# Last opening head unit in halves, low bits by a shift, four resident word tiles, and another order of the second product, in a retention and two-MLP kernel

## The chip, the cores and the metric

One core of a Trainium2 chip. The metric is the device time of one launch in microseconds (us). The kernel before was run three times: 565.46, 564.31 and 565.28 us, median 565.28. TensorE is PE below, its weight load PEld, VectorE DVE, ScalarE ACT, SyncE SP; SP issues most of the transfers.

## The reference

All in fp32, on 2 batches, 8 heads, 768 steps, 64 channels a head; then on 1536 tokens of 512, with 2048 hidden units in each MLP.

```python
for t in range(S):                                   # a decay for each head
    state = gamma * state + einsum('bhd,bhe->bhde', k[:, :, t], v[:, :, t])
    y[:, :, t] = scale * einsum('bhd,bhde->bhe', q[:, :, t], state)
x = y.transpose(0, 2, 1, 3).reshape(1536, 512)
h = x @ moe_w_in;  x = softplus(h) @ moe_w_out       # the first MLP
h = x @ moe2_w_in; x = (h * clip(h + 3, 0, 6) / 6) @ moe2_w_out   # the second
```

## The kernel before, in words

**Exact products from rounded parts.** PE multiplies a rounded fp32 type. Each fp32 operand is cut into a high part (rounded, a copy on ACT) and a low part (what is left, a subtraction on DVE), and each product is three matmuls into one PSUM bank: w high by x high, w high by x low, w low by x high.

**Weights.** A weight tile comes as pairs of 32-bit words (class `Words`, l. 344 to 403). `fetch` loads 512 KB into a `raw` slot by SP. Then `made` (l. 392) records these steps: `bits` (ACT: the low bits of the first words, by an activation), `sign` (ACT), `scale` (ACT) with `clamp` (DVE), or `scaled` and `capped` (both DVE) in their place, and `merge` (DVE). The result is a tile of words in a `cv` slot. `weight` (l. 405) goes on with `high` (ACT) and `low` (DVE) into a `w` slot. The 32 tiles of the first MLP are numbered in the order of their use: in0, in1, in2, out0 (number 3), in3, out1, in4, out2 and so on; `BY_ACT(n)` (l. 180) says which have `scale` on ACT. The first eight in-tiles have their words stored to DRAM (256 KB each) and loaded again by `early_in` (l. 480), for sums of weights that later products use.

**Retention.** `attend` (l. 610) makes one head unit of 128 steps of one batch: load k, q, v; transpose k and q (PE); `kT` (ACT) and `qT` (DVE); `vs` (DVE); the scores (16 matmuls into two banks); two masks (DVE, `pw`); the product of `vs` and k for the state `st`; `carry` (what the state gives); the copy `seen` (DVE), which stands between `carry` and the inner product into the same banks; `inner` (16 matmuls); and the split into `x_hi` (ACT) and `x_lo` (DVE). Units 0 to 3 (START is 4) are the opening; they make the first 512 tokens (c = 0). The other units run in pairs between the matrix products.

**The MLP.** `gemm1` (l. 858) makes 128 hidden rows of 512 tokens, 12 matmuls; for its first step G1(0) all of x high runs ahead of all of x low. ACT copies the bank to `g`, softplus gives `hi` (ACT) and `lo` (DVE). `gemm2` (l. 996) adds the products with a tile of `w_out` into four banks: 4 groups of three matmuls. G1(n) and G2(n) below are the n-th of each. For c = 1 and 2, and in the second MLP, sums of weights and of tokens are multiplied instead, by a scheme with fewer products.

**The order.** Nothing is issued where it stands in the code. `Plan` (l. 25 to 136) is a list planner: each step is a task with an engine, a cost, a due time, the slots it takes and gives, and for a transfer a load on the queue. It runs the tasks in a simulated time; the engine that can start first takes, among its tasks that can start then, the one due first. All instructions are recorded by one line, so every row of the profile says L45, and tiles are told apart by name. A change to one cost can move steps anywhere.

Of the kernel before, what the change touches and what calls it, by code (L numbers as in the profile page):

```python
# [10 lines left out]
F32 = mybir.dt.float32  # L11
# [7 lines left out]
P = 128  # L19
# [126 lines left out]
def kernel(ctx, tc, q, k, v, w1_in, w1_out, w2_in, w2_out, table, out):  # L146
# [33 lines left out]
    def BY_ACT(n):  # L180
        return n < 4 or n >= 16

# [161 lines left out]
    class Words:  # L344


        def __init__(self, m, key, src, inside=0):
            self.m, self.key, self.src = m, key, src
            self.raw_k, self.cv_k = (f"raw{m}", key), (f"cv{m}", key)

        def raw(self):
# [39 lines left out]

        def made(self, at, fetch_at, load, give, by_act=False, hold=0.0):
# [12 lines left out]
    def weight(o, f, number):  # L405
# [204 lines left out]
    def attend(u):  # L610
# [47 lines left out]

        def ps(x):
            return slice(x * NP // parts, (x + 1) * NP // parts)  # L660

        def turned(n, x):
            def go():
                for p in range(NP)[ps(x)]:
                    nc.tensor.transpose(bank((n + "P", u))[:, p, :], tile_of(n)[:, 2 * p:2 * p + 2, :].rearrange("s h d -> s (h d)"), ident)
# [5 lines left out]
        for x in range(parts):  # L671
            at = x and 0.1
            tp = task("PE", cost["Tk"] / parts, turned("k", x), [ik[x], ready.get(("S", u - 2))], d["Tk"] + at, take=[] if x else [("bank", ("kP", u))])
            kt.append(task("ACT", ACP if parts == 1 else act(NP * C // parts, True), lambda x=x: nc.scalar.activation(tile_of("kT")[:, ps(x)], bank(("kP", u))[:, ps(x)], AF.Copy), [tp], d[S] - 1.0 + at,
                           take=[] if x else own("kT"), give=[("kP", u)]))
            tp = task("PE", cost["Tq"] / parts, turned("q", x), [iq[x], ready.get(("C", u - 2))], d["Tq"] + at, take=[] if x else [("bank", ("qP", u))], give=[("q", u)])
            qt.append(task("DVE", PSX if parts == 1 else dve(NP * C // parts), lambda x=x: nc.vector.tensor_tensor(tile_of("qT")[:, ps(x)], bank(("qP", u))[:, ps(x)], tq_sb[:, ps(x)], ALU.mult), [tp, ready["q"]],
                           d[S] - 1.1 + at, take=[] if x else own("qT"), give=[("qP", u)]))
# [57 lines left out]

        s = [task("PE", cost["S0"] / parts, lambda x=x: all_scores(x), [kt[x], qt[x]], d["S"] + x / 10, take=[] if x else [("bank", x) for x in sc], give=[("kT", u)] + [("qT", u)] * first) for x in range(parts)]
        pt = [task("DVE", PSX, masked(g), s, d["I"] - 1.8 + g * 0.6, take=[] if g else own("pw"), give=[sc[g]]) for g in range(2)]
        dp = task("PE", cost["D0"], product, [vs, *ik], d["D"], take=[("bank", dk)], give=[("k", u)])
# [4 lines left out]
        else:  # L744
# [3 lines left out]
            n = task("DVE", 0.1, between, [c], d["C"] + 0.5)  # L748
        c = task("PE", cost["I0"], inner, pt + [vs, n], d["I"], take=[("bank", y) for y in o] if first else [],
                 give=[("pw", u), ("vs", u)])  # L750
        def x_at(part):
            return x_of(part, 0)[:, :, u * C:(u + 1) * C].rearrange("p (y i) t -> p y i t", y=2)

        need = min(due["G1", 0], d["I"] + 12.0)
        o2 = task("ACT", PSX, lambda: nc.scalar.activation(x_at("hi"), split_out(), AF.Copy), [c], need - 1.5, give=o)
        o3 = task("DVE", PSX, lambda: nc.vector.tensor_tensor(x_at("lo"), split_out(), x_at("hi").bitcast(F32), ALU.subtract), [o2],
                  need - 0.8, give=o)
        ready["x", u] = [o2, o3]

# [98 lines left out]
    def gemm1(s):  # L858
# [7 lines left out]

        def go(only=(0, 1)):
            h = at_slot(("h", s))
            w = at_slot(("w", (m, 0, f))).rearrange("p a (k n) -> p a k n", k=KD)
            ops = [(kk, a, b) for kk in range(KD) for a, b in ((0, 0), (0, 1), (1, 0))]  # L870
            for n, (kk, a, b) in enumerate(sorted(ops, key=lambda x: x[2]) if s == 0 else ops):
                if b in only:
                    nc.tensor.matmul(h, w[:, a, kk, :], x_part(kk, b), start=(n == 0), stop=(n == 3 * KD - 1))
# [122 lines left out]
    def gemm2(s):  # L996
# [238 lines left out]
```

## Time and profile before

| | before |
|---|---|
| median of three runs | 565.28 us (564.31 to 565.46) |
| the profiled execution | 564.72 us, of it the span 562.8 |
| PE busy | 553.3 us, 98% |
| PE weight load busy | 473.3 us, 84% |
| DVE busy | 440.5 us, 78% |
| ACT busy | 367.1 us, 65% |
| granted clock of PE | 1.00 over the span |
| transfers | 100.51 MB, 179 GB/s |

The span is the profiled part of the execution, and 1.9 us lie around it. A group's row in the page tells how long its engine was idle just before its instructions, and which engine's instruction or which transfer ended that idle time. Times in the timelines are from the span's start. Matmuls overlap: a row of 12 ends later than the next one starts, so spacing is read from start to start.

### The profile page before, as it was taken

How to read it: one execution, taken by the hardware profiler on the slowest of the kernel's cores; microseconds unless marked ns; L12 is line 12 of the kernel's file. 1: busy time of each engine (PE TensorE's matmuls, PEld its weight loads, DVE VectorE, ACT ScalarE, POOL GpSimd, SP SyncE). 2: the span in 40 equal slices, each digit the busy share in tenths (PEclk: the TensorE clock that was granted, in tenths of full speed). 3: DMA queues.
4: the chain of work that ended last, by engine and by line, in shares of the span. 5: the costliest groups of instructions: out<-in, count | busy, mean ns of one | idle time of the engine just before them, and what ended most of it. 6: DMA issues, size and time to landing. Idle time of an engine off the chain costs nothing.

```text
span 562.8 us, 9577 instructions
## 1 busy us (share of the span) xinstructions
PE 553.3 (98%) x3685; PEld 473.3 (84%) x3685; DVE 440.5 (78%) x778; ACT 367.1 (65%) x600; POOL 5.8 (1%) x13
## 2 busy tenths in 40 slices
PE   8899999999999999999999999999999999999996
PEld 6687788888788888888888999988998889988895
DVE  5999998889799778999998775837887897854443
ACT  4697999997774536687968734448778775432220
POOL 0000000000000000000000000000000000000000
PEclk9999999999999999999999999999999999999999
DMA  9997999994422216988907522243755752236003
GB/s 208 286 238 257 285 294 285 324 236 158 151 75 76 75 62 205 323 305 281 358 21 279 187 75 76 82 180 112 229 183 186 272 177 76 75 106 231 1 0 113
DMA packets 80829, 100.51 MB, mean 179 GB/s; under 512 B 41360, under 2 KB 58000, under 8 KB 80784
## 3 DMA queue, kind: packets, MB, share of 16 engines
q1 hardware_dynamic: 79776, 98.45, 54.3%
q0 software_dynamic: 720, 1.31, 1.3%
q8 instruction: 29, 0.48, 0.3%
q10 hardware_dynamic: 288, 0.14, 0.1%
q14 instruction: 16, 0.13, 0.1%
HBM read 74.98 MB, written 23.59 MB: 175 GB/s over the span
## 4 chain that ended last, share of the span: by engine, by line
PE 82%; DVE 5%; ACT 5%; DMA 5%; issue 1%; DVEq 0%; ACTq 0%; SPq 0%
PE banks L45 82%; DMA raw<-in_moe_w_in_dram 3%; ACT cv L45 2%; DMA raw<-in_moe_w_out_dram 1%; DVE g L45 1%; DVE cv L45 1%; DVE raw L45 1%; DVE lo L45 1%; DMA stash_out<-raw 1%; ACT hi L45 1%; ACT raw L45 0%; DVE qT L45 0%; DMA out_dram<-ob 0%; ACT between L45 0%; ACT w L45 0%
## 5 line engine op out<-in xcount | busy, mean ns | idle before, releaser
L45 PE MATMUL banks<-w,parts 128*128 128x512 f32 x579 | 136.7, 390 | 0.0
L45 PEld LDWEIGHTS banks<-w,parts 128*128 128x128 f32 x579 | 108.0, 188 | 21.3
L45 PE MATMUL banks<-hi,w 128*128 128x512 f32 x384 | 124.8, 393 | 0.0
L45 PE MATMUL banks<-xf,w 128*128 128x384 f32 x672 | 123.2, 337 | 0.4 <-DVE c L45 0.4
L45 PEld LDWEIGHTS banks<-xf,w 128*128 128x128 f32 x672 | 118.3, 188 | 3.4 <-DVE c L45 0.7
L45 PEld LDWEIGHTS banks<-hi,w 128*128 128x128 f32 x384 | 72.1, 188 | 15.0
L45 PE MATMUL banks<-xl,w 128*128 128x512 f32 x342 | 81.0, 391 | 0.2
L45 PEld LDWEIGHTS banks<-xl,w 128*128 128x128 f32 x342 | 63.7, 188 | 14.1 <-DVE hs L45 0.5
L45 PE MATMUL banks<-lo,w 128*128 128x512 f32 x192 | 75.1, 391 | 0.2 <-DVE lo L45 0.2
L45 ACT ACTIVATE e<-c,three 128x384 f32<-128x384 f32 (+1 forms) x32 | 24.6, 770 | 47.0 <-DVE c L45 46.5
L45 ACT ACTIVATE cv<-raw,half 128x512 uint32<-128x512 uint32 x64 | 48.6, 761 | 7.5 <-DMA raw<-in_moe_w_out_dram 3.7
L45 ACT ACTIVATE cv<-raw 128x512 f16<-128x512 int32 x64 | 50.0, 788 | 1.2
L45 DVE SCALAR_TENSOR_TENSOR cv<-raw,cv 128x512 uint32<-128x512 uint32 x64 | 44.1, 690 | 1.4
L45 PE MATMUL banks<-x_hi,w 128*128 128x512 f32 x128 | 42.5, 399 | 1.0 <-ACT x_hi L45 1.0
L45 PEld LDWEIGHTS banks<-lo,w 128*128 128x128 f32 x192 | 36.1, 188 | 7.9 <-DVE lo L45 0.9
L45 DVE TENSOR_SCALAR raw<-raw 128x512 f32<-128x512 f32 x76 | 32.3, 430 | 11.4 <-ACT raw L45 10.5
L45 ACT ACTIVATE hi<-g 128x512 fp32r<-128x512 f32 x48 | 29.9, 626 | 16.7 <-PE banks L45 10.1
L45 DVE TENSOR_TENSOR lo<-g,hi 128x512 fp32r<-128x512 f32 x48 | 33.0, 688 | 8.0 <-ACT hi L45 7.8
L45 ACT ACTIVATE parts<-c 128x768 fp32r<-128x768 f32 x32 | 26.9, 842 | 18.6 <-DVE c L45 18.6
L45 DVE TENSOR_TENSOR parts<-c,parts 128x768 fp32r<-128x768 f32 x32 | 30.6, 957 | 10.2 <-ACT parts L45 9.9
L45 ACT ACTIVATE e<-e 128x512 f32<-128x512 f32 x48 | 29.7, 624 | 9.3 <-DVE e L45 9.2
L45 ACT ACTIVATE raw<-raw 128x512 f32<-128x512 f32 x52 | 34.4, 668 | 0.7
(95 smaller groups left out, 653.5 us busy)
## 6 DMA issues: line engine op xcount, KB each, us to landing
raw<-in_moe_w_in_dram SPq DMA_DIRECT2D x32, 512.0 KB, 5.6
raw<-in_moe_w_out_dram SPq DMA_DIRECT2D x32, 512.0 KB, 5.7
w<-stash_out SPq DMA_DIRECT2D x32, 512.0 KB, 5.4
stash_out<-raw SPq DMA_DIRECT2D x16, 512.0 KB, 3.4
w<-parts_out SPq DMA_DIRECT2D x14, 512.0 KB, 5.4
parts_out<-w SPq DMA_DIRECT2D x8, 512.0 KB, 4.3
stash_h<-hs SPq DMA_DIRECT2D x16, 256.0 KB, 2.3
g<-stash_h SPq DMA_DIRECT2D x16, 256.0 KB, 4.6
```

Of the source, the lines that this page charges most:

```text
L45: return self.plan.tc.keep_in_program_order(getattr(self.engine, op)(*args, **kwargs))
```

## The change

It has five parts. (1) The last opening unit (u = 3) is made in halves: scores, masks, inner product, `x_hi` and `x_lo`; G1(0)'s part of x high runs in two steps of four matmuls. (2) Tiles 3 to 11 and 16 to 31 get their low bits by a shift on DVE (`shifted`) and not by ACT's `bits`; all tiles have `scale` on ACT. (3) The words of in0 to in3 stay in four SBUF tiles (`words`); their stores and reloads go. (4) In `gemm2` the three products come as (w high, hi), (w low, hi), (w high, lo), and for c = 0 as two PE tasks: eight matmuls that read hi, four that read lo. (5) The planner's loads for k, q, v and the raw tiles get other values, and those of later units another hold.

```diff
+    RESIDENT = 4
...
+    MEASURED = {"k": (1.2, 1.2, 1.2, 0.9), "q": (1.2, 1.1, 1.1, 1.15), "v": (2.1, 0.75, 1.4, 2.3)}
...
     def BY_ACT(n):
-        return n < 4 or n >= 16
+        return True
+
+    def SHIFTED(n):
+        return n>=3 and n<12 or n>=16
...
+            self.stays = key[:2] == (0, 0) and key[2] < RESIDENT
+            self.home = "words" if self.stays else f"cv{m}"
...
+        def shifted(self):
+            nc.vector.tensor_scalar(self.w(), self.raw()[:, :, 0], 29, None, ALU.logical_shift_right)
...
-            t1 = nc.add("ACT", 0.65, self.bits, [t0], at - 3.5, take=[(f"cv{self.m}", self.cv_k)])
+            t1 = nc.add(*(("DVE", TS, self.shifted) if shifted else ("ACT", 0.65, self.bits)), [t0], at - 3.5, take=[(self.home, self.cv_k)])
...
-        t5 = x.made(use - tail, begin + 15 if number < 1 else use - tail - 8.0, 1.45 if o else 1.5 if number < EARLY else 1.75, [x.raw_k], BY_ACT(number))
+        t5 = x.made(use - tail, begin + 15 if number < 1 else use - tail - 8.0, 1.45 if o else (2.1, 1.9, 1.4)[number] if number < EARLY else 1.6, [x.raw_k], BY_ACT(number), shifted=SHIFTED(number))
...
-        if not o and f // 2 in PAIRS:
+        if x.stays:
+            T["S", key] = t5
+        elif not o and f // 2 in PAIRS:
...
+        if 2 * p < RESIDENT:
+            words_k = [("cv0", (0, 0, 2 * p + f)) for f in range(2)]
+            forms(0, p, lambda f: at_slot(words_k[f]).bitcast(F32), [T["S", (0, 0, 2 * p + f)] for f in range(2)], words_k, at)
+            return
...
-                         load=(1.25 if u < START else 1.32) / parts, hold=HOLD + when if u >= START else 0.0) for j in range(parts)]
+                         load=(MEASURED[n][u] if u < START else 1.1) / parts, hold=HOLD + when - 4 * (u >= START + 2) if u >= START else 0.0) for j in range(parts)]
...
+        cut = 2 if u == START - 1 else 1
...
+        def masked_both(x):
+            def go():
+                a = nc.slot[sc[0]][1]
+                nc.vector.tensor_tensor(tile_of("pw")[:, :, ps(x)], banks[:, a:a + 2, :].rearrange("p g (n t) -> p g n t", n=NP)[:, :, ps(x)],
+                                        full.rearrange("p (g n t) -> p g n t", g=1, n=1).to_broadcast([P, 2, NP // cut, C]), ALU.mult)
+            return go
...
-        def inner():
-            for n in range(H):
+        def inner(x):
+            for n in range(x * H // cut, (x + 1) * H // cut):
...
+            c = task("PE", cost["I0"] / cut, lambda x=x: inner(x), (pt[x:x + 1] if cut == 2 else pt) + [vs, c], d["I"] + x / 10, take=[("bank", y) for y in o] if first else [],
+                     give=[("pw", u), ("vs", u)])
+            o2 = task("ACT", PSX if cut == 1 else act(NP * C // 2, True), high, [c], need - 1.5 + x / 10, give=o)
+            o3 = task("DVE", PSX if cut == 1 else dve(NP * C // 2), low, [o2], need - 0.8 + x / 10, give=o)
+            if cut == 2:
+                o2.ahead = .8
...
-            p = nc.add("PE", GEMM * 2 / 3, lambda: go([0]), T["W", (m, 0, f)] + [a for u in range(START) for a in ready["x", u][:1]], at, take=w_take)
+            p = None
+            for y in range(2):
+                p = nc.add("PE", GEMM / 3, lambda y=y: go([0], range(2 * y, 2 * y + 2)), T["W", (m, 0, f)] + [p] + [a for u in range(START) for a in ready["x", u][::2][y if u == START - 1 else 0:][:1]], at + y / 20, take=[] if y else w_take)
...
-                for n, (l, r) in enumerate(((wh, hi), (wh, lo), (wl, hi))):
+                for n, (l, r) in list(enumerate(((wh, hi), (wl, hi), (wh, lo))))[of.start:of.stop]:
...
+        if f != ORDER[c][-1] and c == 0:
+            take = [("bank", ("acc", c, j)) for j in range(KD)] if f == ORDER[c][0] else []
+            p = nc.add("PE", GEMM * 2 / 3, lambda: go(range(KD), range(2)), [t for t in deps if t is not T["g", s][1]], at, take=take)
+            T["acc", c] = [nc.add("PE", GEMM / 3, lambda: go(range(KD), range(2, 3)), deps + [p], at + 0.1, give=give)]
+            return
```

How it moves instructions, at three places. A number behind a name tells tiles of one name apart; the numbers differ between the two kernels.

**First place: the last opening unit on DVE and ACT, 21 to 28 us.** On DVE, before, from `vs` of the unit (`vs_1`) on; `x_lo` in the second row is that of the unit before:

```order
L45 TENSOR_TENSOR vs_1_148<-v_3_152,small 128x512
L45 TENSOR_TENSOR x_lo_309<-banks,x_hi_297 128x4x128
L45 TENSOR_TENSOR pw_0_149<-banks,small 128x512 x2
L45 COPY seen<-banks 128x2
L45 TENSOR_TENSOR st_169<-st_168,banks 128x256
L45 TENSOR_SCALAR raw_1_69<-raw_1_69 128x512
L45 SCALAR_TENSOR_TENSOR cv_1_74<-raw_1_69,cv_1_74 128x512
```

and with the change:

```order
L45 TENSOR_TENSOR vs_1_144<-v_3_148,small 128x512
L45 TENSOR_TENSOR pw_0_145<-banks,small 128x2x256 x2
L45 COPY seen<-banks 128x2
L45 TENSOR_TENSOR x_lo_313<-banks,x_hi_303 128x4x128
L45 TENSOR_TENSOR st_165<-st_164,banks 128x256
L45 TENSOR_TENSOR st_165<-st_165,small 128x256
L45 TENSOR_TENSOR x_lo_313<-banks,x_hi_303 128x2x128 x2
L45 TENSOR_SCALAR cv_0_73<-raw_3_71 128x512
```

The `x_lo` of the unit before goes behind the masks and `seen`, the masks cover half of both banks each, and the unit's own `x_lo` runs in halves, ahead of the work on weight in1 (`raw_1`).

On ACT, before, from the unit's `kT` on (`w_78` is the high part of in1, `raw_2` in2, `raw_3` out0):

```order
L45 ACTIVATE kT_1_144<-banks 128x512
L45 ACTIVATE x_hi_297<-banks 128x4x128
L45 ACTIVATE cv_1_74<-raw_1_69,half 128x512
L45 ACTIVATE cv_1_74<-raw_1_69 128x512
L45 ACTIVATE raw_1_69<-raw_1_69 128x512
L45 ACTIVATE cv_2_75<-raw_2_70,half 128x512
L45 ACTIVATE cv_2_75<-raw_2_70 128x512
L45 ACTIVATE x_hi_297<-banks 128x4x128
L45 ACTIVATE w_78<-cv_1_74 128x512
L45 ACTIVATE raw_2_70<-raw_2_70 128x512
```

and with the change:

```order
L45 ACTIVATE kT_1_140<-banks 128x512
L45 ACTIVATE x_hi_303<-banks 128x4x128
L45 ACTIVATE words_435<-raw_1_69,half 128x512
L45 ACTIVATE words_435<-raw_1_69 128x512
L45 ACTIVATE x_hi_303<-banks 128x2x128 x2
L45 ACTIVATE raw_1_69<-raw_1_69 128x512
L45 ACTIVATE words_465<-raw_2_70,half 128x512
L45 ACTIVATE words_465<-raw_2_70 128x512
L45 ACTIVATE w_78<-words_435 128x512
L45 ACTIVATE raw_2_70<-raw_2_70 128x512
L45 ACTIVATE cv_0_73<-raw_3_71 128x512
L45 ACTIVATE raw_3_71<-raw_3_71 128x512
```

`x_hi` of the last unit goes ahead of the scale of in1 (`raw_1`), and both bits and sign of in2 behind it; out0 (`raw_3`) has no bits step here.

**Second place: the first product with `w_out` on PE, 32 to 42 us, and the work on its weight on DVE.** On PE, before (`w_79` is in2, `w_81` in3, `w_80` out0; `hi_94` and `lo_96` are the softplus of G1(0)):

```order
L45 MATMUL banks<-x_hi_297,w_81 128x512 x2
L45 MATMUL banks<-x_lo_309,w_81 128x512
L45 MATMUL banks<-x_hi_297,w_81 128x512
L45 MATMUL banks<-ident,k_1_138 128x128 x4
L45 MATMUL banks<-hi_94,w_80 128x512
L45 MATMUL banks<-lo_96,w_80 128x512
L45 MATMUL banks<-hi_94,w_80 128x512 x2
L45 MATMUL banks<-lo_96,w_80 128x512
```

and with the change:

```order
L45 MATMUL banks<-x_hi_303,w_79 128x512 x2
L45 MATMUL banks<-x_lo_313,w_79 128x512
L45 MATMUL banks<-x_hi_303,w_79 128x512
L45 MATMUL banks<-hi_94,w_80 128x512 x8
L45 MATMUL banks<-lo_96,w_80 128x512 x4
L45 MATMUL banks<-ident,k_1_134 128x128 x4
L45 MATMUL banks<-x_hi_303,w_81 128x512
L45 MATMUL banks<-x_lo_313,w_81 128x512
```

G2(0), eight matmuls of `hi` and four of `lo`, goes ahead of G1(3) (`w_81`) and of the transposes of `k_1`. On DVE, with the change (`raw_3` out0, `raw_0` out1, `raw_2` in2, `words_482` in3):

```order
L45 TENSOR_SCALAR words_482<-raw_4_72 128x512
L45 TENSOR_TENSOR w_78<-words_435,w_78 128x512
L45 TENSOR_SCALAR raw_2_70<-raw_2_70 128x512
L45 SCALAR_TENSOR_TENSOR words_465<-raw_2_70,words_465 128x512
L45 TENSOR_SCALAR cv_1_74<-raw_0_68 128x512
L45 TENSOR_SCALAR raw_3_71<-raw_3_71 128x512
L45 TENSOR_TENSOR w_79<-words_465,w_79 128x512
L45 SCALAR_TENSOR_TENSOR cv_0_73<-raw_3_71,cv_0_73 128x512
L45 TENSOR_SCALAR e_90<-g_91 128x512
```

The shifts of in3 and of out1 are the TENSOR_SCALAR rows that write `words_482` and `cv_1_74`; before, DVE had no such rows.

**Third place: DVE at 434 us.** Before:

```order
L45 SCALAR_TENSOR_TENSOR cv_3_76<-raw_0_68,cv_3_76 128x512
L45 SCALAR_TENSOR_TENSOR cv_2_75<-raw_1_69,cv_2_75 128x512
L45 TENSOR_SCALAR raw_2_70<-raw_2_70 128x512
L45 SCALAR_TENSOR_TENSOR cv_0_73<-raw_2_70,cv_0_73 128x512
L45 TENSOR_TENSOR c_3197<-total_3199,banks 128x384
L45 TENSOR_TENSOR raw_0_68<-cv_3_76,raw_0_68 128x512
L45 SCALAR_TENSOR_TENSOR c_3197<-e_0_3182,c_3197 128x384
```

and with the change:

```order
L45 SCALAR_TENSOR_TENSOR cv_2_75<-raw_1_69,cv_2_75 128x512
L45 TENSOR_SCALAR raw_2_70<-raw_2_70 128x512
L45 TENSOR_TENSOR c_3189<-total_3192,banks 128x384
L45 SCALAR_TENSOR_TENSOR cv_0_73<-raw_2_70,cv_0_73 128x512
L45 SCALAR_TENSOR_TENSOR c_3189<-e_0_3173,c_3189 128x384
L45 TENSOR_TENSOR c_3226<-part_3162,banks 128x384 x2
```

The step c<-total goes ahead of the merge into `cv_0`.

## Rows read from the trace of the kernel before

**Rows 1.** The page, part 1: busy us (share of the span) xinstructions, TensorE's line.
```profile
PE 553.3 (98%) x3685; PEld 473.3 (84%) x3685; DVE 440.5 (78%) x778; ACT 367.1 (65%) x600; POOL 5.8 (1%) x13
```

**Rows 2.** Busy time by stretch: busy us (instructions) per engine, PE's granted clock, DMA share, GB/s.
```profile
30.00:40.00 10.00, 10.00 (x52) 8.15 (x51) 9.43 (x20) 9.82 (x18) 0.00 (x0) 1.00 1.01 259
60.00:75.00 15.00, 15.00 (x76) 12.47 (x75) 14.79 (x29) 14.36 (x26) 1.51 (x2) 1.00 1.04 274
```

**Rows 3.** Timeline of PE, 23 to 33 us: start, us, engine, out<-in, [idle before <-releaser].
```profile
23.12 0.69 PE L45 MATMUL banks<-vs,k 128*64 128x64 f32 x16
24.19 1.09 PE L45 MATMUL banks<-pw,vs 128*64 128x128 f32 x16 [0.38 <-DVE seen L45]
26.31 2.11 PE L45 MATMUL banks<-x_hi,w 128*128 128x512 f32 x8 [1.03 <-ACT x_hi L45]
...
29.17 0.39 PE L45 MATMUL banks<-x_hi,w 128*128 128x512 f32 x1
...
31.89 0.60 PE L45 MATMUL banks<-ident,k 128*128 128x128 f32 x4
...
32.68 0.48 PE L45 MATMUL banks<-x_hi,w 128*128 128x512 f32 x1
```

**Rows 4.** Timeline of DVE, 22 to 24 us.
```profile
22.18 0.69 DVE L45 TENSOR_TENSOR x_lo<-banks,x_hi 128x512 fp32r<-128x512 f32 x1
22.79 1.28 DVE L45 TENSOR_TENSOR pw<-banks,small 128x512 f32<-128x512 f32 x2
```

**Rows 5.** Timeline of ACT, 3 to 29 us.
```profile
3.86 0.38 ACT L45 ACTIVATE kT<-banks 128x256 f32<-128x256 f32 x1 [1.38 <-PE banks L45]
...
22.84 0.79 ACT L45 ACTIVATE cv<-raw 128x512 f16<-128x512 int32 x1
23.66 0.67 ACT L45 ACTIVATE raw<-raw 128x512 f32<-128x512 f32 x1
...
25.70 0.56 ACT L45 ACTIVATE x_hi<-banks 128x512 fp32r<-128x512 f32 x1
26.16 0.62 ACT L45 ACTIVATE w<-cv 128x512 fp32r<-128x512 f32 x1
26.68 0.68 ACT L45 ACTIVATE raw<-raw 128x512 f32<-128x512 f32 x1
27.24 0.77 ACT L45 ACTIVATE cv<-raw,half 128x512 uint32<-128x512 uint32 x1
28.04 0.79 ACT L45 ACTIVATE cv<-raw 128x512 f16<-128x512 int32 x1
28.70 0.62 ACT L45 ACTIVATE w<-cv 128x512 fp32r<-128x512 f32 x1
```

**Rows 6.** Timeline of PE, 49 to 51 us.
```profile
49.99 0.51 PE L45 MATMUL banks<-hi,w 128*128 128x512 f32 x1
50.70 0.50 PE L45 MATMUL banks<-lo,w 128*128 128x512 f32 x1 [0.20 <-DVE lo L45]
```

**Rows 7.** Groups: engine op out<-in shapes xcount, busy us, mean ns, idle before us <-releasers.
```profile
L45 PEld LDWEIGHTS banks<-lo,w 128*128 128x128 f32 x192 | 36.1, 188 | 7.9 <-DVE lo L45 0.9
...
L45 DVE TENSOR_SCALAR e<-g 128x512 uint32<-128x512 uint32 x48 | 20.1, 422 | 1.0 <-ACT g L45 0.8
```

**Rows 8.** Timeline, 435 to 436 us.
```profile
435.10 0.55 DVE L45 TENSOR_TENSOR c<-total,banks 128x384 f32<-128x384 f32 x1
...
435.70 0.61 PE L45 MATMUL banks<-xf,w 128*128 128x384 f32 x2 [0.41 <-DVE c L45]
```

**Rows 9.** Timeline, 71 to 75 us.
```profile
71.88 0.68 DVE L45 TENSOR_TENSOR w<-cv,w 128x512 fp32r<-128x512 f32 x1
...
74.34 0.48 PE L45 MATMUL banks<-x_hi,w 128*128 128x512 f32 x1
```

**Rows 10.** Timeline of SP's DMA issues, 19 to 20 us.
```profile
19.22 0.98 SPq L45 DMA_DIRECT2D raw<-in_moe_w_out_dram  x1
```

**Rows 11.** DMA issues in that stretch: line engine op xcount, KB each, median us to landing.
```profile
raw<-in_moe_w_out_dram SPq DMA_DIRECT2D x1, 512.0 KB, 10.2
```

More of the change, by code (lines that the diff above doesn't have):

```diff
@@ L241 @@
     slots["raw1"], slots["cv1"] = slots["raw0"], slots["cv0"]
+    nc.pool("words", RESIDENT)
+    slots["words"], kinds["words"] = {}, ([P, CH], U32)
     room("w", SLOTS - LATE, [P, 2, CH], F32R, later=[("arena", j) for j in range(LATE)])
@@ L390, in merge, with made @@
             nc.vector.scalar_tensor_tensor(self.w(), self.y(), 3, self.w(), ALU.logical_shift_left, ALU.bitwise_or)
-        def made(self, at, fetch_at, load, give, by_act=False, hold=0.0):
+        def made(self, at, fetch_at, load, give, by_act=False, hold=0.0, shifted=False):
             T["F", self.key] = t0 = nc.add("SP", 0.45, self.fetch, due=fetch_at, take=[(f"raw{self.m}", self.raw_k)], load=load, hold=hold)
-            t1 = nc.add("ACT", 0.65, self.bits, [t0], at - 3.5, take=[(f"cv{self.m}", self.cv_k)])
+            t1 = nc.add(*(("DVE", TS, self.shifted) if shifted else ("ACT", 0.65, self.bits)), [t0], at - 3.5, take=[(self.home, self.cv_k)])
             if self.m or by_act:
@@ L657, in attend, with ps @@
             ready["q"] = nc.add("ACT", ACP, lambda: nc.scalar.activation(tq_sb, bank(("tqP", 0)), AF.Copy), [t], begin, give=[("tqP", 0)])
-        def ps(x):
-            return slice(x * NP // parts, (x + 1) * NP // parts)
+        cut = 2 if u == START - 1 else 1
+        def ps(x, cut=max(parts, cut)):
+            return slice(x * NP // cut, (x + 1) * NP // cut)
         def turned(n, x):
             def go():
-                for p in range(NP)[ps(x)]:
+                for p in range(NP)[ps(x, parts)]:
                     nc.tensor.transpose(bank((n + "P", u))[:, p, :], tile_of(n)[:, 2 * p:2 * p + 2, :].rearrange("s h d -> s (h d)"), ident)
@@ L673, in attend @@
             tp = task("PE", cost["Tk"] / parts, turned("k", x), [ik[x], ready.get(("S", u - 2))], d["Tk"] + at, take=[] if x else [("bank", ("kP", u))])
-            kt.append(task("ACT", ACP if parts == 1 else act(NP * C // parts, True), lambda x=x: nc.scalar.activation(tile_of("kT")[:, ps(x)], bank(("kP", u))[:, ps(x)], AF.Copy), [tp], d[S] - 1.0 + at,
+            kt.append(task("ACT", ACP if parts == 1 else act(NP * C // parts, True), lambda x=x: nc.scalar.activation(tile_of("kT")[:, ps(x, parts)], bank(("kP", u))[:, ps(x, parts)], AF.Copy), [tp], d[S] - 1.0 + at,
                            take=[] if x else own("kT"), give=[("kP", u)]))
             tp = task("PE", cost["Tq"] / parts, turned("q", x), [iq[x], ready.get(("C", u - 2))], d["Tq"] + at, take=[] if x else [("bank", ("qP", u))], give=[("q", u)])
-            qt.append(task("DVE", PSX if parts == 1 else dve(NP * C // parts), lambda x=x: nc.vector.tensor_tensor(tile_of("qT")[:, ps(x)], bank(("qP", u))[:, ps(x)], tq_sb[:, ps(x)], ALU.mult), [tp, ready["q"]],
+            qt.append(task("DVE", PSX if parts == 1 else dve(NP * C // parts), lambda x=x: nc.vector.tensor_tensor(tile_of("qT")[:, ps(x, parts)], bank(("qP", u))[:, ps(x, parts)], tq_sb[:, ps(x, parts)], ALU.mult), [tp, ready["q"]],
                            d[S] - 1.1 + at, take=[] if x else own("qT"), give=[("qP", u)]))
@@ L686, in attend, with split_out @@
             return
-        def split_out():
+        def split_out(ys):
             a = nc.slot[o[0]][1]
-            return banks[:, a:a + 2, :NP // 2 * C].rearrange("p y (i t) -> p y i t", i=NP // 2)
+            return banks[:, a + ys.start:a + ys.stop, :NP // 2 * C].rearrange("p y (i t) -> p y i t", i=NP // 2)
         dk = ("ds", u)
@@ L735, in faded @@
                                     tc_sb.rearrange("p (n o) -> p n o", o=1).to_broadcast([P, NP, D]), ALU.mult)
-        s = [task("PE", cost["S0"] / parts, lambda x=x: all_scores(x), [kt[x], qt[x]], d["S"] + x / 10, take=[] if x else [("bank", x) for x in sc], give=[("kT", u)] + [("qT", u)] * first) for x in range(parts)]
-        pt = [task("DVE", PSX, masked(g), s, d["I"] - 1.8 + g * 0.6, take=[] if g else own("pw"), give=[sc[g]]) for g in range(2)]
+        n = max(parts, cut)
+        s = [task("PE", cost["S0"] / n, lambda x=x: all_scores(x), [kt[x % parts], qt[x % parts]], d["S"] + x / 10, take=[] if x else [("bank", x) for x in sc], give=[("kT", u)] + [("qT", u)] * first) for x in range(n)]
+        pt = [task("DVE", PSX, masked_both(g) if cut == 2 else masked(g), [s[g]] if cut == 2 else s, d["I"] - 1.8 + g * 0.6, take=[] if g else own("pw"), give=sc if cut == 2 else [sc[g]]) for g in range(2)]
         dp = task("PE", cost["D0"], product, [vs, *ik], d["D"], take=[("bank", dk)], give=[("k", u)])
@@ L748, in attend, with x_at, high, low @@
             n = task("DVE", 0.1, between, [c], d["C"] + 0.5)
[L749 to L752, printed above, removed]
+        ready["x", u] = []
         need = min(due["G1", 0], d["I"] + 12.0)
[L755 to L758, printed above, removed]
+        c = n
+        for x in range(cut):
+            ys = slice(x, x + 1) if cut == 2 else slice(0, 2)
+            def x_at(part, ys=ys):
+                return x_of(part, 0)[:, :, u * C:(u + 1) * C].rearrange("p (y i) t -> p y i t", y=2)[:, ys]
+            def high(x_at=x_at, ys=ys):
+                nc.scalar.activation(x_at("hi"), split_out(ys), AF.Copy)
+            def low(x_at=x_at, ys=ys):
+                nc.vector.tensor_tensor(x_at("lo"), split_out(ys), x_at("hi").bitcast(F32), ALU.subtract)
+            c = task("PE", cost["I0"] / cut, lambda x=x: inner(x), (pt[x:x + 1] if cut == 2 else pt) + [vs, c], d["I"] + x / 10, take=[("bank", y) for y in o] if first else [],
[4 more added lines that the diff above has]
+                o2.ahead = .8
+            ready["x", u] += [o2, o3]
     def pair(u, task):
@@ L865, in x_part, with go @@
             return at_slot(("xl", forms_of[kk // 2]))[:, b, kk % 2] if c else x_of(("hi", "lo")[b], 0)[:, kk, :]
-        def go(only=(0, 1)):
+        def go(only=(0, 1), those=range(KD)):
             h = at_slot(("h", s))
@@ L871, in go @@
             for n, (kk, a, b) in enumerate(sorted(ops, key=lambda x: x[2]) if s == 0 else ops):
-                if b in only:
+                if b in only and kk in those:
                     nc.tensor.matmul(h, w[:, a, kk, :], x_part(kk, b), start=(n == 0), stop=(n == 3 * KD - 1))
@@ L1000, in gemm2, with go @@
         deps = T["W", w_key if w_key[0] == "wl" else w_key[1]] + T["g", s] + T.get(("acc", c), [T["last product"]] if c == NC - 1 else [])
-        def go(js):
+        def go(js, of=range(3)):
             wh, wl = (at_slot(w_key)[:, i] for i in range(2))
-            hi, lo = at_slot(("hi", s)), at_slot(("lo", s))
+            hi = at_slot(("hi", s))
+            lo = at_slot(("lo", s)) if of.stop == 3 else hi
             for j in js:
                 sl = slice(j * P, (j + 1) * P)
-                for n, (l, r) in enumerate(((wh, hi), (wh, lo), (wl, hi))):
+                for n, (l, r) in list(enumerate(((wh, hi), (wl, hi), (wh, lo))))[of.start:of.stop]:
                     nc.tensor.matmul(at_slot(("acc", c, j)), l[:, sl], r, start=(f == ORDER[c][0] and n == 0), stop=(f == ORDER[c][-1] and n == 2))
         give = [("hi", s), ("lo", s), w_key]
+        if f != ORDER[c][-1] and c == 0:
[3 more added lines that the diff above has]
+            return
         if f != ORDER[c][-1]:
```

## The prediction

> **What bounds the kernel now.** I read the page's busy table first: TensorE (PE) is busy for 553.3 of 562.8 us [rows 1], so a time can only come out of the 9.5 us in which it idles, or go into new idle time. Then I read the timeline of PE for its gaps. Before 21 us the change touches only the order of unit 0's and unit 1's work. The last head unit and the first matrix products are in [rows 3]: 16 inner products start at 24.19 after an idle 0.38 that the copy `seen` on VectorE (DVE) ended, and G1(0), the first product with `w1_in`, starts at 26.31 after an idle 1.03 that `x_hi` on ScalarE (ACT) ended. G1(0) holds PE until 29.17 (2.86), G1(1) until 31.89 (2.72), that is 12 matmuls at 0.227 each, and unit 4's transposes until 32.68 (0.79). Behind that PE is full: 10.00 of 10 us and 15.00 of 15 [rows 2]. In the same stretches ACT has 9.82 of 10 and 14.36 of 15, DVE 9.43 and 14.79. Three engines are full at once there, and the reader should keep that in mind: what PE wins at 26 us it keeps only if ACT and DVE deliver weights and activations earlier as well.
>
> **The opening.** *Masks.* Before, unit 2's `x_lo` (22.18 to 22.79 in steps of DVE's queue) stands between `vs` and the two masks [rows 4]. The change puts it behind them, so the masks start at 22.18 and not 22.79, and are done at 22.18 + 1.28 = 23.46. The inner product then waits no longer for `seen` but for the product of `vs` and k ahead of it on PE, which starts at 23.12 and is 0.69 long [rows 3]: 23.81. I take 23.8 for 24.19, so 0.39 earlier.
>
> *Halves.* The first half of the inner product is 0.55 (half of 1.09 [rows 3]), done at 24.35; ACT's step of 0.05 behind it gives 24.40. ACT then moves 128x256 and not 128x512. A move of 128x256 out of PSUM took 0.38 (`kT` at 3.86), one of 128x512 0.56 [rows 5]. So x_hi's first half is there at 24.78, and G1(0) starts at 24.83 and not 26.31: **1.48 earlier**, done at 24.83 + 2.86 = 27.69. x_lo's halves are wanted eight matmuls later (26.65), and DVE has them by about 25.8. The price of two moves is 0.76 against 0.56 on ACT. [...]
>
> *G1(1).* It needs weight in1, and ACT's steps come in this order: x_hi's halves (24.40, 24.94), scale(in1) 25.2, bits(in2) 25.76, sign(in2) 26.56, high(in1) 27.22. I use ACT's steps from start to start, from [rows 5]: a weight's high part 0.52 (26.16 to 26.68), scale 0.56 (26.68 to 27.24), bits 0.80 (27.24 to 28.04), sign 0.66 (28.04 to 28.70), or 0.82 where its own scale follows (22.84 to 23.66), a move out of PSUM 0.46 (25.70 to 26.16). DVE's low part of in1 follows at 27.87 and takes 0.69: 28.56. The third matmul of G1(1) reads it, and ten more steps of 0.227 give 30.85 in place of 31.89: **1.04 left**.
>
> *The first product with `w1_out`.* The change puts G2(0) ahead of G1(3) and of the next transposes on PE. Its operand hi0 comes late in ACT's queue. I go on by the same steps: high(in1) 27.22, scale(in2) 27.74, sign(out0) 28.30, scale 29.12, high(in2) 29.68, g0 30.20, sign(in3) 30.68, scale 31.50, high(out0) 32.06, g1 32.58, e0 33.06, high(in3) 33.58, sign(out1) 34.10, hi0 34.76, done 35.4. PE comes to it at 30.85 + 0.79 + 2.84 (G1(2)) = 34.48. So a **new stall of about 0.95** stands there, and of the 1.04 no more than 0.1 to 0.4 is left when G2(1) starts. The bounds of this term are all of it (nothing left) and none of it (1.04 left, if ACT runs ahead of my steps by 1 us over 19 instructions). I take 0.1, by the steps.
>
> **The second product.** Before, each group of three runs (wh,hi), (wh,lo), (wl,hi), so `lo` is wanted by the second matmul. PE's second matmul of one such product starts 0.71 behind its first (49.99, 50.70), which is 0.48 more than the step of 0.227 [rows 6]. Over the whole kernel weight loads idle 0.9 for lo [rows 7]; the rest of the 0.9 is at 59 us. The change runs eight matmuls of the high part first, 8 x 0.227 = 1.8 us, before lo is read. DVE's lo takes 0.69 after hi, so both waits go if hi is in time, as it was. That is a gain of 0.8 to 0.9, and with the 0.1 from the opening **1.0 by 61 us**. The nearest rows that bound it are 0 (lo is only late because hi is) and 0.9.
> The weight that is loaded changes with each matmul in the new order. The trace has 3685 loads for 3685 matmuls [rows 1] already, and a load is 188 ns beside a step of 227 [rows 7, 3], so the order costs nothing. [...]
>
> **DVE at 435 us.** PE idles 0.41 for `c` at 435.70, and DVE's step c<-total runs at 435.10 [rows 8]. A merge stands directly ahead of it in DVE's queue; the change has them the other way round. A two-source step of this size holds the queue 0.61 (22.18 to 22.79 [rows 4]). The gain is between 0.41 and 0.61; I take **0.5**.
>
> **Costed at nothing.** *Shifts.* 25 tiles (3 to 11 and 16 to 31) lose ACT's bits (0.80) and get a shift on DVE. The trace has no such shift. The nearest row is a bit operation with a constant on as many words, 422 ns [rows 7]; two-source operations of the size are 0.69 [rows 4]. I take 0.42, the same kind of instruction, with 0.42 and 0.69 as bounds. Tiles 4 to 11 trade it for DVE's second pass of the same price, and ACT pays scale for bits, about -0.1 each. Tiles 12 to 15 pay ACT a scale more (0.56 each), and DVE one pass less; there ACT has the least room (2% to 4% idle [rows 2]). The cover is the lead of weights: in8's low part is done at 71.88 + 0.68 = 72.56, and its product starts at 74.34 [rows 9], 1.8 early. Four times 0.56 would be 2.2, so at the worst 0.4 comes through. From tile 16 on ACT wins 0.8 and DVE pays 0.42 each, with PE waiting for neither. *Resident words.* Four stores and four reloads of 256 KB go. PE waited for none of them; what they leave free is DMA time. *Other order* in units 0 and 1: the same instructions, 0 to 0.1.
>
> **Sum.** 0.1 + 0.9 + 0.5 and 0.1 for small things is 1.6. The profiled execution took 564.72, so 563.1; it lies 0.56 under the median of the runs (565.28), and I put half of that on: **563.4**.
>
> **Rivals.** *ACT sets the pace.* If ACT's queue, not PE, decides when G2(0) to G2(3) can run, then the lo waits turn into waits for hi, and tiles 12 to 15 cost their 0.4. What is left is the 0.5 at 435 us and 0.1 or so: 564.1 to 564.7. For it speaks ACT's 98% and 96% [rows 2], against it that hi of the third product was there before PE.
> *All of it is kept.* If ACT runs about 1 us ahead of my steps, 1.0 more is kept at G2(0), and small gaps of 0.2 to 0.4 elsewhere close: up to 3.6 in all. It gives 561.1 to 562.3. Against it stands the order, in which hi0 has 14 ACT steps behind high(in1).
> *Slower: DVE's queue stops at a shift.* A shift reads words as they land, and DVE runs its queue in order; before, ACT alone met a late word. Now out1's shift stands ahead of out0's clamp, in2's low part and out0's merge. DVE reaches out1's at about 29.5; before, out1 was issued at 19.22 [rows 10] and took 10.2 [rows 11]: 29.4. From the shift on, DVE has four steps to out0's merge (0.42 + 0.36 + 0.61 + 0.61 = 2.0), and ACT wants out0's high part at 32.06. So the point is a landing at 30.0: each us behind that holds out0's high part, hi0 behind it on ACT, and PE, a us for a us. The time is then 563.4 plus the landing less 30.0; one at 32 gives 565.4, one at 33.4 (4 us later than before) 566.8. For it: a load that takes 10.2 has no transfer time to itself, and the loads around it change places. Against it: no store of words is left to share them.
>
> **Chances.** Forecast 0.50, with 562.3 to 564.0 (of it 0.10 within the bound); ACT's pace 0.22 (0.18 within); all kept 0.13; DVE stops 0.15 (0.10 slower, 0.05 within). A measurement of this kernel can tell 0.2%, or 1.13 us, from no change: faster is below 564.15. Faster 0.40 + 0.04 + 0.13 = 0.57, same 0.10 + 0.18 + 0.05 = 0.33, slower (above 566.41) 0.10. The range goes from 561.1 (all kept) to 565.4 (DVE stopped for 2 us).
>
> **What would show it.** G1(0) starts near 24.8 with x_hi's first half as the last releaser; G1(1) ends near 30.9; a stall of about 1 us stands before G2(0) with hi as the releaser; no wait for lo is left before 61 us; no wait for c near 435. I am wrong if the gap before G2(0) is missing or over 2 us, if DVE shows an idle stretch before a shift with a transfer as releaser, or if PE waits for weights between 60 and 110 us.

## The result, and the profile after

The changed kernel takes 571.3 us (median of 4 runs, 570.72 to 571.95) against 564.79 for the kernel before, measured beside it: a ratio of 1.0115, 95% interval 1.0097 to 1.0134. It is slower by 6.5 us; 563.4 was forecast, with 561.1 to 565.4 as the range.

The page of the changed kernel, part 1; PE has the same work and 6.9 us more span [rows 1]:

```profile
span 569.7 us, 9547 instructions
...
PE 554.6 (97%) x3685; PEld 474.1 (83%) x3685; DVE 443.4 (78%) x792; ACT 357.2 (63%) x588; POOL 5.9 (1%) x13
```

What PE waited for, over the span (us in total, times, longest). Kernel before:

```profile
PE banks L45 <- DVE qT L45: 2.0, 3, 0.9
...
PE banks L45 <- ACT x_hi L45: 1.0, 1, 1.0
PE banks L45 <- DVE c L45: 0.4, 1, 0.4
PE banks L45 <- DVE seen L45: 0.4, 1, 0.4
PE banks L45 <- DVE lo L45: 0.2, 1, 0.2
```

Changed kernel:

```profile
PE banks L45 <- DVE qT L45: 3.9, 4, 2.2
PE banks L45 <- DVE st L45: 2.4, 1, 2.4
PE banks L45 <- DVE vs L45: 1.4, 1, 1.4
...
PE banks L45 <- ACT hi L45: 1.0, 2, 0.6
PE banks L45 <- DMA k<-in_k_dram: 0.5, 1, 0.5
PE banks L45 <- DVE seen L45: 0.2, 1, 0.2
```

The waits for x_hi, c and lo are gone, as the change meant; waits for st, vs, hi and a transfer of k are new, and there is a longer one for qT. Their places, PE's timeline of the changed kernel (start us, us, ..., idle before and its releaser):

```profile
9.06 0.69 PE L45 MATMUL banks<-vs,k 128*64 128x64 f32 x16 [1.37 <-DVE vs L45]
...
24.14 1.09 PE L45 MATMUL banks<-pw,vs 128*64 128x128 f32 x16 [0.25 <-DVE seen L45]
25.28 2.11 PE L45 MATMUL banks<-x_hi,w 128*128 128x512 f32 x8
...
31.38 0.60 PE L45 MATMUL banks<-ident,k 128*128 128x128 f32 x4
...
35.81 2.11 PE L45 MATMUL banks<-hi,w 128*128 128x512 f32 x8 [0.64 <-ACT hi L45]
...
58.20 2.12 PE L45 MATMUL banks<-hi,w 128*128 128x512 f32 x8 [0.39 <-ACT hi L45]
...
92.45 0.39 PE L45 MATMUL banks<-x_hi,w 128*128 128x512 f32 x1
...
102.57 0.65 PE L45 MATMUL banks<-ident,k 128*128 128x128 f32 x4 [2.23 <-DVE qT L45]
...
105.77 1.16 PE L45 MATMUL banks<-qT,kT 64*64 64x64 f32 x64 [0.21 <-DVE qT L45]
...
117.26 2.17 PE L45 MATMUL banks<-pw,vs 64*64 64x64 f32 x61 [2.43 <-DVE st L45]
...
309.96 1.23 PE L45 MATMUL banks<-xf,w 128*128 128x384 f32 x6
```

The same steps in the kernel before, which tell how far behind PE is:

```profile
92.25 0.39 PE L45 MATMUL banks<-x_hi,w 128*128 128x512 f32 x1
...
302.62 0.69 PE L45 MATMUL banks<-xf,w 128*128 128x384 f32 x3
```

At 92 us PE is 0.2 late, at 310 us 7.3 late, at the end 6.9. So nearly all of it, 7.1, is lost between 92 and 310 us, and the timeline has it at two places before 125 us. DVE's timeline there, changed kernel:

```profile
94.63 0.42 DVE L45 TENSOR_SCALAR cv<-raw 128x512 uint32<-128x512 uint32 x1
98.41 0.43 DVE L45 TENSOR_SCALAR cv<-raw 128x512 uint32<-128x512 uint32 x1 [3.35 <-DMA words_in<-cv]
98.75 0.68 DVE L45 TENSOR_TENSOR vs<-v,small 128x512 f32<-128x512 f32 x1
...
101.83 0.68 DVE L45 TENSOR_TENSOR qT<-banks,tq_sb 128x512 f32<-128x512 f32 x1
...
115.01 0.43 DVE L45 TENSOR_SCALAR cv<-raw 128x512 uint32<-128x512 uint32 x1 [2.29 <-DMA w<-cv]
115.35 0.94 DVE L45 TENSOR_TENSOR st<-st,banks 128x256 f32<-128x256 f32 x2
```

Both stops are shifts (of out10 and of out12). Each waits not for the words that it reads but for the slot that it writes: an earlier tile's words are still being read there. The words that out10's shift reads were issued at 88.80 and took 6.0, so they were there at 94.8; its slot was read until 97.9 by a store to DRAM, and until 97.7 by the accumulating transfer that makes a low part (`w<-cv`, issued by GpSimd). At the second stop it is an accumulating transfer alone. Behind the shifts in DVE's queue stand qT and st, for which PE waits 2.23 and 2.43 us. In the kernel before, neither DVE nor ACT waits for a transfer between 60 and 130 us. The text ahead of the prediction says that eight in-tiles have their words stored; the trace has 14 such stores, and ten are left in the changed kernel, all behind 40 us. How long the two transfers of the stops took (DMA issues of 89 to 90 us and of 105 to 108 us; KB each, median us to landing):

```profile
words_in<-cv SPq DMA_DIRECT2D x1, 256.0 KB, 8.5
...
w<-cv POOLq DMA_DIRECT2D x1, 256.0 KB, 8.4
```

In the code, `Plan` counts such a store as a load of 0.8 on the queue and such an accumulating transfer as 1.6.

After the second stop PE also ran slower. Busy time by stretch (the column before the DMA share is the granted clock):

```profile
117.00:118.00 1.00, 0.61 (x18) 0.48 (x22) 0.93 (x3) 0.18 (x1) 0.00 (x0) 0.97 0.35 73
118.00:120.00 2.00, 2.00 (x87) 2.00 (x82) 1.97 (x5) 0.18 (x1) 0.00 (x0) 0.50 0.85 230
120.00:122.00 2.00, 2.00 (x19) 1.59 (x13) 1.66 (x5) 2.00 (x4) 0.00 (x0) 0.66 0.84 293
122.00:124.00 2.00, 2.00 (x10) 1.62 (x10) 1.97 (x5) 0.56 (x2) 0.87 (x1) 1.00 1.13 310
```

The granted clock is 0.50, the lower of the two levels that this trace has on record (1.00 and 0.50), from about 118 to 121 us; it fell some 0.7 us after PE had come back from its idle 2.43. It costs about 2.0: 1.5 on the head unit's small matmuls (117.26 to 120.32, where the kernel before took 1.55) and 0.5 on the next. From start to start PE lost 2.4 + 0.3 + 2.5 + 2.0 = 7.2 here (the expectations below reckon with 7.4), and won 0.4 near 441 us (435 us before).

### The profile page after: what moved, and what is told of

Same layout as the page of the kernel before. It is cut to its first block, busy times and chain, and to the rows that moved or that the text cites. A ratio compares the mean times of both kernels' runs of the same rounds, so it can differ in the third digit from the quotient of the medians.

```text
span 569.7 us, 9547 instructions
## 1 busy us (share of the span) xinstructions
PE 554.6 (97%) x3685; PEld 474.1 (83%) x3685; DVE 443.4 (78%) x792; ACT 357.2 (63%) x588; POOL 5.9 (1%) x13
## 4 chain that ended last, share of the span: by engine, by line
PE 81%; DVE 7%; DMA 6%; ACT 4%; issue 1%; SPq 1%; DVEq 0%; ACTq 0%
PE banks L45 81%; DMA words_in<-cv 2%; DMA w<-cv 1%; DVE cv L45 1%; ACT cv L45 1%; DMA v<-in_v_dram 1%; DVE w L45 1%; ACT raw L45 1%; ACT w L45 1%; DVE st L45 1%; DVE raw L45 1%; SPq L45 1%; DVE lo L45 1%; DMA k<-in_k_dram 0%; DVE vs L45 0%
## 5 line engine op out<-in xcount | busy, mean ns | idle before, releaser
L45 PE MATMUL banks<-hi,w 128*128 128x512 f32 x384 | 112.5, 393 | 1.0 <-ACT hi L45 1.0
L45 PE MATMUL banks<-lo,w 128*128 128x512 f32 x192 | 67.8, 391 | 0.0
L45 ACT ACTIVATE cv<-raw 128x512 f16<-128x512 int32 x60 | 46.8, 787 | 1.0 <-DVE cv L45 0.3
L45 ACT ACTIVATE raw<-raw 128x512 f32<-128x512 f32 x64 | 42.4, 670 | 0.9
L45 DVE SCALAR_TENSOR_TENSOR cv<-raw,cv 128x512 uint32<-128x512 uint32 x60 | 41.1, 689 | 1.2
L45 DVE TENSOR_TENSOR c<-total,banks 128x384 f32<-128x384 f32 x16 | 8.9, 554 | 34.4 <-PE banks L45 34.4
L45 ACT ACTIVATE w<-cv 128x512 fp32r<-128x512 f32 (+1 forms) x49 | 28.4, 588 | 10.0 <-DVE cv L45 9.7
```

Of the source, the lines that this page charges most:

```text
L45: return self.plan.tc.keep_in_program_order(getattr(self.engine, op)(*args, **kwargs))
```

## The experiments

Theory A: a shift stands in DVE's queue until its slot is free (3.35 and 2.29 us above), and DVE's other work waits behind it (PE had qT's transposes done at 96.4, and qT started at 101.83). Rival B: the loads of k, q, v come sooner and crowd the transfers; the shift only shows it. Rival C: the time would come back elsewhere. Each ratio below is to the kernel before, run beside it.

**own_two.** Two tiles of words get memory of their own, so that nobody has to wait for the slot; the order of every engine stays that of the changed kernel.

```diff
+    OWN, own_words = ((0, 1, 10), (0, 1, 12)), {}
...
         def w(self):
+            if self.key in OWN:
+                if self.key not in own_words:
+                    own_words[self.key] = hold.tile([P, CH], U32, name="own%d" % self.key[2])
+                return own_words[self.key]
             return at_slot(self.cv_k)
```

> The words of out10 and out12 get SBUF tiles of their own; every engine keeps the order of the changed kernel. Theory A (a shift on DVE waits until the slot it writes is free of a store and an accumulating transfer, 3.35 us before out10's and 2.29 us before out12's, and PE runs dry): both stops go, and with them PE's gaps of 2.4, 0.4 and 2.6 us and the 2.0 us at the lower granted clock behind the second: 571.3 less 7.4 is 563.9, between 563.0 and 565.0. Rival B (the transfers themselves are late, because k, q, v of later units are loaded 4 us sooner; the shift only shows it): the next late transfer holds DVE or PE at the same places, 568 or more. Rival C (the lost time comes back as a wait for weights or for hi between 100 and 125 us): 566 to 568.

Measured: 565.15 us, 1.0017 of before (1.0004 to 1.003). Both stops are gone, and with them 0.98% of the 1.15%, 5.5 us. DVE's longest wait for a transfer between 86 and 125 us is this one:

```profile
97.49 0.43 DVE L45 TENSOR_SCALAR own<-raw 128x512 uint32<-128x512 uint32 x1 [0.17 <-DMA raw<-in_moe_w_out_dram]
```

Theory A is shown for this order; C falls, and B's 568 is not reached. What is left, +1 us, is not the gain forecast, and the time lies just above A's range.

**own_one.** The same for out10 alone.

> Only out10's words get a tile of their own; the order is that of the changed kernel. Theory A: the stop of 3.35 us goes (2.4 + 0.4 of PE), the one of out12 stays with its 2.6 us gap and about 2.0 us at the lower clock: 571.3 less 2.8 is 568.5, between 567.5 and 569.5. Were the clock's fall tied to both gaps, 566.5. Rival B: no change, 570.5 or more.

Measured: 566.61 us, 1.0068 (1.0035 to 1.0102). This is below the range of theory A; its six runs lie between 565.93 and 573.09. In its profile out12's stop was 1.1 and PE idled 0.7 there, without a lower clock behind it. The stop that is left is worth 0.5% here, less than expected, and in the profile it was half as long as in the changed kernel. The time is the one named for a clock that falls with both gaps only, but with a gap of 0.7 in place of 2.4 that isn't tested.

**bits_two.** out10 and out12 get their low bits from ACT again; PE and SP keep their order; on DVE and ACT the planner moves some other rows too.

```diff
     def SHIFTED(n):
-        return n>=3 and n<12 or n>=16
+        return n>=3 and n<12 or n>=16 and n not in (23, 27)
```

> out10 and out12 get their low bits on ACT again, by the activation of before, so ACT and not DVE waits for the slots; PE and SP keep the order of the changed kernel. Theory A: ACT idles 2 to 3 us for the slots, with work of other tiles behind it; DVE runs on to qT and st: 564 to 567. Rival B: PE still runs dry for late transfers, 568 or more.

Measured: 566.74 us, 1.0039 (1.0023 to 1.0055), in the range of theory A, but not with its sign, an idle 2 to 3 us on ACT. Neither DVE nor ACT stands for a slot over 0.2 us between 60 and 130 us: when ACT came to these tiles, their slots were free.

**old_loads.** The planner's loads and holds are those of before; the rest is the change, and the order is planned anew.

```diff
-                         load=(MEASURED[n][u] if u < START else 1.1) / parts, hold=HOLD + when - 4 * (u >= START + 2) if u >= START else 0.0)
+                         load=(1.25 if u < START else 1.32) / parts, hold=HOLD + when if u >= START else 0.0)
```

> The planner's loads and holds for k, q, v and the raw tiles are those of before; shifts, halves, resident words and the product order stay. Theory A: DVE still meets slots whose store or accumulation is under way, at the same or other tiles, stops of 1 to 4 us: 566 to 573. Rival B: the stops are gone, 563 to 565.

Measured: 564.55 us, 1.0012 (0.9997 to 1.0027): the time that B had. No DVE wait for a transfer is left between 60 and 130 us. But the transfers are no faster: the stores issued at 85.33 and 86.38 us took 6.7 and 8.7, and the slowest one in the kernel before took 9.5. So a store of 8.7 us made no stop by itself here. The stops took both: the shift on DVE, and an order in which its slot is still in use. With either away they are gone: bits_two has no wait for a slot over 0.2 us between 60 and 130 us, old_loads none. Whether the sooner loads or the rest of the new order brought the shifts to slots in use, this run does not tell.

**only_shift, only_halves, only_order, only_loads.** Each makes one part of the change alone in the kernel before (the diffs are those parts of the change). The resident words were not run alone.

> The kernel before with the shifts (tiles 3 to 11 and 16 to 31) and ACT's scale alone; loads, halves, resident words and product order are those of before. If the shift alone makes DVE meet occupied slots (theory A): DVE idles over 1 us for a store or an accumulating transfer between 85 and 120 us, and the time is 1 to 6 us above before's. If it takes the moved loads as well (theory A+B): no such stop, within 1 us of before's.

> The kernel before with the last opening unit in halves alone (and G1(0)'s part of x high in two steps). By the forecast's steps G1(0) starts 1.5 us earlier; what the changed kernel showed is 1.0. If PE keeps it: 1.0 below before's time. If ACT's queue takes it back by 61 us (rival of the forecast): within 0.4 of before's.

> The kernel before with the other order of the three products, and the two steps for c = 0, alone. Forecast: the waits for lo go, 0.9 below before's time. Rival: each wait for lo becomes a wait for hi of 0.4 or more, since ACT sets the pace: within 0.4 of before's.

> The kernel before with the planner's new loads and holds alone. If late transfers by themselves hold the engines (rival B): ACT's bits idle for slots or landings and PE runs dry near 100 us, 2 us or more above before's. If ACT's queue has the slack for the waits (theory A): within 1 us of before's.

Measured: 568.27 (1.0062), 568.26 (1.0064), 568.29 (1.0055) and 570.75 us (1.0091), intervals of 0.0016 to 0.0032 to either side. Every part alone loses 3 us or more. For only_shift and only_loads theory A and rival B named such times, but without the signs that they named: only_shift has no wait for a slot, and in only_loads neither does ACT wait for a transfer nor PE run dry between 60 and 130 us. Each makes the planner write another order: DVE's order differs from that of before in 178 to 244 lines (removed and added ones together, tile numbers left out), of 778 instructions. New waits lie where the part changes nothing, as in PE's timeline of only_halves near 307 us:

```profile
306.62 1.32 PE L45 MATMUL banks<-xf,w 128*128 128x384 f32 x6 [0.35 <-ACT base L45]
308.97 1.33 PE L45 MATMUL banks<-xf,w 128*128 128x384 f32 x6 [1.04 <-DVE part L45]
```

only_shift has no DVE wait over 1 us for a slot; it has one of 1.4 for v and PE's waits of 0.4 and 0.7 at 308 and 315. So these four can't tell what a part is worth. Their orders, planned anew, came with some 3 us or more; that need not be, as old_loads shows (1.0012).

**high_first, x_halves, both_kept.** The same two parts without a new plan: inside a task, so that no other instruction moves.

```diff
-            for j in js:
+            steps = [(j, n) for j in js for n in range(3)]
+            for j, n in sorted(steps, key=lambda x: x[1] == 2) if c == 0 and len(js) == KD else steps:
...
-                for n, (l, r) in enumerate(((wh, hi), (wh, lo), (wl, hi))):
+                for l, r in (((wh, hi), (wl, hi), (wh, lo))[n],):
```

```diff
+        pieces = [slice(y, y + 1) for y in range(2)] if u == START - 1 else [slice(0, 2)]
...
+        def high():
+            for ys in pieces:
+                nc.scalar.activation(x_at("hi")[:, ys], split_out()[:, ys], AF.Copy)
```

> The kernel before, its plan untouched: for c = 0 the twelve matmuls of a product in one PE task run as eight of (w high, hi), (w low, hi) and then four of (w high, lo). No row of any other engine moves. Forecast's term: the two waits for lo (0.48 and 0.29) go, 0.5 to 0.9 below before's time (0.9984 to 0.9991). If ACT's queue sets the pace: within 0.2 us of before's (0.9996 or more).

> The kernel before, its plan untouched: x_hi and x_lo of the last opening unit are two instructions each, in the places of the one; nothing else moves. Forecast's term, without the masks' part: x_hi's first half is there after half of the inner product, G1(0) starts 0.5 to 1.0 us earlier (25.3 to 25.8 for 26.31), kept if w in1 and hi0 are in time: 0.3 to 0.9 below before's time. If ACT's queue takes it back (two moves cost it 0.2): within 0.2 us.

> Both of these in the untouched plan of before. Forecast's terms: 0.8 to 1.6 below before's time (0.997 to 0.9986), faster than both kernels. If ACT sets the pace: within 0.4 us of before's.

Measured: high_first 563.91 us, 0.9991 (0.998 to 1.0003); x_halves 564.48, 1.0005 (0.9993 to 1.0017); both_kept 564.18, 0.9992 (0.9981 to 1.0003). In high_first eight matmuls of hi start at 49.95 and the four of lo follow at 51.90 without a wait [rows 6]; from start to start the two products take 0.47 and 0.31 less than before. The time, 0.5 us lower, is the low end of what was expected, but the interval just holds no change. both_kept was expected at 0.9986 or less and misses it. In x_halves ACT comes to x_hi no sooner (PE's and ACT's timelines):

```profile
26.09 2.14 PE L45 MATMUL banks<-x_hi,w 128*128 128x512 f32 x8 [0.81 <-ACT x_hi L45]
```

```profile
25.04 0.78 ACT L45 ACTIVATE cv<-raw 128x512 f16<-128x512 int32 x1
25.68 0.63 ACT L45 ACTIVATE x_hi<-banks 128x256 fp32r<-128x256 f32 x2
```

A sign step stands ahead until 25.68, so G1(0) wins 0.2, and the total nothing. Behind a busy ACT the halves won 0.2 here; in the changed kernel, where G1(0) came 1.03 earlier, ACT idled 1.14 before x_hi, which was the planner's doing.

**vs_first, vs_late.** vs_first is own_two with `vs` of unit 0 ahead of its masks (`vs.ahead = 1.0` for u = 0; three rows of DVE move). vs_late is the kernel before with `vs` held behind them (`hold=7.4` for u = 0).

> The kernel with two tiles of words of their own (own_two), and in unit 0 vs ahead of both masks on DVE, as before the change; nothing else moves. Theory D (the changed order of unit 0 leaves PE idle 1.4 us near 8 us, and in most executions PE's granted clock stays at its lower level until 9 to 13 us, which costs up to 3 us by 24 us): 1.0 to 2.5 below own_two's 1.0017 of before, so 0.996 to 1.000 of before's time. Forecast's own view (the reorder of units 0 and 1 costs 0 to 0.1): as own_two, 1.001 to 1.003.

> The kernel before with vs of unit 0 behind the masks, and the transposes of unit 1 ahead of unit 0's inner product, as the changed kernel has them; 14 rows on DVE, 6 on PE and 4 on SP move. Theory D: 1 to 2.5 us above before's time, most of it in the first 13 us. The forecast's own view: within 0.3 us.

Measured: vs_first 564.96 us, 1.0016 (0.9999 to 1.0033); vs_late 564.62 us, 1.0009 (0.9998 to 1.002). Neither is as large as theory D had it; some 0.5 us for vs_late is not told from none. The lower clock of theory D is on record only in own_one's profile (0.50 from 10 to 12 us); that most executions have it, no run shows. vs_first shows another thing, in DVE's timeline:

```profile
95.87 0.43 DVE L45 TENSOR_SCALAR own<-raw 128x512 uint32<-128x512 uint32 x1 [2.03 <-DMA raw<-in_moe_w_out_dram]
```

With the slot out of the way, out10's shift waits for its words to land: 2.03 here, 0.2 in the profile of own_two. The transfer took 8.6 here and 6.5 there. DVE stands at the shift for it, and PE then idled 1.2 for qT.

**slots_later.** The planner takes a slot for free 2 us later where a store or an accumulating transfer reads it (`max(u.done + u.tail ...)`, with `tail` 2.0 for these), in the changed kernel.

> The changed kernel, with a planner that takes a slot of words for free 2 us later where a store or an accumulating transfer reads it; the order is planned anew. Theory A: no stop over 1 us of DVE for such a slot, so 563.5 to 566.5 where the new order has no other stop. Rival B (transfers late by themselves): 568 or more.

Measured: 569.45 us, 1.0099 (1.0076 to 1.0123): a miss. A stop of 1.9 for a slot stays, PE idles 1.6 behind it, and new waits for c of 0.8 and 0.6 stand at 317.56 and 442.18 us. The order was planned anew here too, so it doesn't speak for B.

## Why the prediction was wrong, point by point

- **The step that failed** is the rival "DVE's queue stops at a shift". The mechanism was named, but priced at one place (out1, near 30 us) and for one cause, the landing of the words that the shift reads. There DVE did not wait. It waited at 98 and 115 us for the slot that the shift writes, 3.35 and 2.29 us. Under "Costed at nothing" the forecast said of tiles 16 to 31 that PE waits neither for ACT nor for DVE there, and gave no reason; own_two puts 5.5 of the 6.5 us on two of their shifts. What is queued behind an added wait was worked out for one shift of 25. "No store of words is left to share them" held near 30 us, but ten stores are left from 40 us on, and one of them held the first shift. The forecast's own sign of being wrong, an idle stretch of DVE before a shift with a transfer as releaser, is what the trace shows.
- *Masks, 0.39 forecast, 0.05 found* (24.14 for 24.19): the first mask of the unit waited 0.50 for PE and started at 22.73, when all 16 scores were done (21.52 + 1.16 = 22.68), so halved scores gave nothing.
- *Halves:* from inner product to G1(0) 1.14, forecast 1.03. G1(0) started 1.03 earlier, not 1.48; 0.34 of the difference is the masks'. G1(1) ended 0.51 earlier, not 1.04: in1's low part was ready at 28.92, forecast at 28.56.
- *The stall ahead of G2(0)* came as forecast: PE 0.8 late from start to start, released by hi, at 35.81 (about 35.4 forecast).
- *The waits for lo* went, and one for hi took the place of the second (0.39 at 58.20): ACT had stood 0.8 us at 55.70 for a slot whose store took 4.8. That this made hi late is read from ACT's rows and was not tested; the profiles of own_one and own_two, with the same order on PE, don't have this wait. By 61 us the changed kernel had gained nothing, where 1.0 was forecast. The term was taken as 0.9; in high_first, in an order that stays, PE's rows give it 0.8, and the time 0.5, not clear of none.
- *The step c<-total*: the wait went, as forecast, but a wait too short for the table took part of its place; from start to start PE won 0.37, where 0.41 to 0.61 was forecast.
- *A shift's cost*: right, 0.42 (24 of them, mean 420 ns). The other order of the products cost nothing on weight loads, right by the trace (3685 loads as before, busy 474.1 us for 473.3).
- *Units 0 and 1, 0 to 0.1 forecast*: PE idled 1.4 for `vs` at 9.06, mostly made up by 17 us; vs_late puts at most 0.2% on it.
- *What own_two leaves*, 1.0017 where the forecast's sum was 0.997, stays open. Its one profile has G1(0) at 28.30, 2.0 later than before, behind an opening in which the small matmuls took up to 1.8 times as long (unit 0's scores 2.08, 1.16 in the changed kernel); from G1(0) to the end it takes 536.3 us, the kernel before 536.5. With the same order on PE, G1(0) starts at 25.28, 27.04 and 28.30 in the profiles of the changed kernel, own_one and own_two. That is more than the gain forecast for the opening, so one profile can't settle it.

## What to carry to other kernels

An operation that moved to another engine brought waits there, 3.35 and 2.29 us on DVE: besides its inputs, ask of each moved instruction who still reads the memory that it writes, how long that reader (a store, an accumulating transfer) takes in the trace, and what stands behind it in the new queue. Where a planner writes the order, test a part inside the order that is there; a part that makes it plan anew is measured together with the new order (four such parts lost 3.4 to 5.9 us here).

## What was not expected

With four different parts an order planned anew came with a loss of 3 to 6 us, and with old_loads with none to speak of. PE's idle of 2.43 us at 115 us was followed by some 3 us at the lower granted clock; the idle of 2.23 at 100 us was not. In the opening, the 16 score matmuls of unit 0 took 1.16 us in one profile and 2.08 in another (own_two) of the same order, with a granted clock of 1.00 on record in both; in own_one 0.50 is on record from 10 to 12 us. Why is open.
